# One block of an MLP product moved into the attention products, its second half packed in pairs, a fixed order, and two first loads on ScalarE's queue

## The chip, the cores and the metric

The kernel runs on one core of a Trainium2 chip. The metric is the device time in microseconds. The core's engines are TensorE (PE, matrix products; PEld is its weight load), VectorE (DVE), ScalarE (ACT), GpSimd (POOL) and SyncE (SP), which here issues the transfers (DMAs).

## The reference, cut to what matters

```python
def _A_ref(x, wqkv, wo):              # S=2048, D=512, H=32 heads of 16, W=8, dil=2
    qkv = (x @ wqkv) ...
    off = jnp.arange(W) * dil         # a token sees itself and 7 others, 2 apart
    logits = jnp.einsum("bhsd,bhswd->bhsw", q, kg) * scale
    ...
    o = jnp.einsum("bhsw,bhswd->bhsd", attn, vg)
    return o.transpose(...).reshape(B, S, D) @ wo
def _B_ref(x, w1, b1, w2, b2):        # F = 1376 = 10*128 + 96
    y = _layernorm(x, axis=-1)
    h = _gelu(jnp.einsum("bsd,df->bsf", y, w1) + b1)
    return jnp.einsum("bsf,fd->bsd", h, w2) + b2
x = A_x
xn = _layernorm(x, axis=-1)
s = _A_ref(xn, A_wqkv, A_wo)
g = _silu(_B_ref(xn, B_w1, B_b1, B_w2, B_b2))
return x + s * g
```

All inputs and outputs are float32.

## The kernel before, in words

Every operand of a product is split into two 16-bit parts, high and low, and a product is three matmuls: high by high, low by high, high by low. With the inner dimension of 512 in four parts of 128, a tile of an output takes 12 matmuls.

The 2048 tokens are taken as two parities c (a window with dilation 2 stays within one), each of 8 tiles of 128 tokens. First x is loaded, normalized, split and transposed to yT, some tiles by PE (line 683) and some by a transposing DMA (line 675). For two tiles ("FP", 6 and 7) a transposed copy of x is loaded too (line 1124, called t6 and t7), centred (a reduce on DVE at line 602, a small product at 608, a subtraction at 610), and multiplied by head block 0's weights in float32 directly (line 617), before anything is split.

The attention comes in 8 units: parity c by head block hb (8 heads, 384 columns of q, k and v). A unit's products (line 746) make 8 tiles of 12 matmuls into the product banks ps; ACT (line 763) or DVE (759) scales each out into U. DMAs copy halo rows of U (line 771), then DVE multiplies q by k (805), reduces (808), makes the softmax, multiplies by v (863, in the last unit 901), adds (858), and ACT and DVE split the result into high and low (846, 848); DMAs transpose it into oT (851). The output product with wo is line 929 for the first parity and line 961 for the last, whose results DVE scales and adds to x (993, 1000).

The MLP runs in 4 chunks (ch) of 512 tokens by NF = 11 blocks of F, the last of them 96 wide. The first product (mlp1, line 1016) makes a block transposed, features on partitions, in 12 matmuls of 512 columns; ACT does the gelu (1033) and the high part (1036), DVE the low part (1038). The second product (mlp2, line 1052) adds the block to four banks z, 3 matmuls each. The last block's h lies in a tile of its own, hlast, 97 rows: 96 features and a row that carries the bias b2. ACT's silu of z (1068, last chunk 1063) gives g, which goes through DRAM (gd) to the end.

The weights are brought to 16 bit at run time: loads (head blocks: load_q, line 505), sums of squares (514), a power of two as scale (qsc for head block 0), high parts (536) and low parts (543). At the start, small products of a constant tile (line 1169) keep PE busy.

A list scheduler in the class Plan sets the order on every engine: the code adds operations with an engine, an estimated duration, a priority and what they read and write, and the loop repeatedly places the one that the priorities and estimated times choose. Constants at the head of the file (priorities P..., engine choices such as HI_ENG, the order of the loads LOADS) feed it. Each engine then executes its list in that order.

Of the kernel before, what the change touches and what calls it, by code (L numbers as in the profile page):

```python
# [8 lines left out]
F32 = mybir.dt.float32  # L9
# [9 lines left out]
P = 128  # L19
# [14 lines left out]
LASTPOOL = (0, 2, 4)  # L34

# [3 lines left out]
LAG = 2  # L39

# [4 lines left out]
BYDMA = (4, 5, 6, 7)  # L45
TRZ = (3, 3, 0, 2, 0, 1, 1, 0)
PTR = (0.5487, 0.3388, 0.0342, 0.6565, 0.7826, 0.1978, 0.0549, 0.9)
GROUPS = ((0,), (1, 2), (3, 4, 5), (6, 7))
BATCHES = ((0, 1, 2, 3, 4, 5), (6, 7))
LOADS = (('t', 6), ('q', 0), ('q', 2), ('x', 2), ('x', 0), ('q', 4), ('t', 7), ('x', 5), ('x', 1), ('x', 3), ('x', 4), ('q', 6), ('w', 0), ('w', 2), ('x', 7), ('c', 2), ('s', 1), ('c', 0), ('w', 3), ('x', 6), ('w', 1), ('c', 1), ('b', 0), ('s', 0))  # L50
HI_ENG = ('act', 'act', 'act', 'dve', 'dve', 'dve', 'dve', 'act')
XT = (0, 4, 30, 34)
Y_ENG = ('pool', 'act', 'dve', 'dve', 'act', 'pool', 'dve', 'act')

W1ENG = ('act', 'dve', 'act', 'act', 'act', 'act', 'act')
# [3 lines left out]
W2LO = ('dve', 'dve', 'dve', 'dve', 'dve', 'pool', 'dve')  # L59
EV0 = ('act', 'dve', 'dve', 'act', 'act', 'act', 'dve', 'dve')  # L60
EV1 = ('dve', 'dve', 'act', 'act', 'act', 'act', 'dve', 'act')
QLO0 = ('pool', 'dve', 'dve', 'pool')
QLO1 = ('dve', 'dve')
W1LO = ('dve', 'dve', 'pool', 'dve', 'dve', 'dve', 'dve')
WOLAG = 2
MEANBY = ('dve', 'pe', 'pool', 'pool')
W2LATE = 6

BEFORE_W1 = (0, 1, 4, 5)

# [26 lines left out]
class Plan:  # L97
# [9 lines left out]
    def add(self, eng, dur, fn, reads=(), writes=(), prio=None, table=None, nbytes=0,  # L107
            after=None, holds=(), port=False, rate=350e3, issue=0.55, tail=1.4):
# [56 lines left out]
    def start(self):  # L165
        for o in self.ops:
            o.npred, o.ready, o.succs = len(o.preds), 0.0, []
        for o in self.ops:
            for p in o.preds:
                p.succs.append(o)  # L170
        self.free = {o.eng: 0.0 for o in self.ops}
        self.portfree, self.dma, self.landed, self.table = 0.0, 0.0, [], None

    def earliest(self, o):
        t = max(self.free[o.eng], o.ready)
        if o.port:
            t = max(t, self.portfree)
        if o.eng == "sp" and o.nbytes:
            left = FLIGHT
            for end, n in reversed(self.landed):  # L180
                left -= n
                if left < 0:
                    t = max(t, end)
                    break
        return t

    def place(self, o, t):

        if o.eng == "sp":
# [3 lines left out]
            self.dma = max(self.dma, t + o.issue + 0.3)  # L193
            self.dma += o.nbytes / (o.rate if self.dma > SLOW else 265e3)
            end = self.dma + o.tail
            self.landed.append((end, o.nbytes))
            return end
        end = t + o.dur
        if o.nbytes:
            self.free[o.eng] = end  # L200
            self.dma = max(self.dma, end + 0.3) + o.nbytes / o.rate
# [20 lines left out]
    def issue(self):  # L222
# [55 lines left out]
SLOW = 5.5  # L278

FLIGHT = 0.9e6  # L280

PW2 = 1.1284
PS2 = 0.4252
PWQ1 = 0.9
PW1 = 0.423
PB1 = 0.75
PCS = 0.6
PQ0 = 0.2677
PSQ0 = 0.1788
PMEAN = 0.04  # L290
PDIR = (0.192, 0.1517, 0.1187, 0.1556)
PG = (0.5671, 0.5205, 0.3952, 0.4033)
PY = (0.8339, 0.1477, 0.3649, 0.4824, 0.05, 0.5767, 0.05, 0.8333)
PU0 = 0.8687
PU1 = 0.969
PWARM = 0.9
PEV = 0.2698

PTOT = 0.5899

WAKE = 24
PS1 = 1.1561
# [3 lines left out]
PQLO = 0.5225  # L306

PFPLN = 0.35
PSEC = (0.6153, 0.7518, 0.1)

U1MH = 4
# [5 lines left out]
IORD0 = (6, 7, 0, 4, 1, 3, 2, 5)  # L317
IORD1 = (7, 0, 6, 3, 2, 4, 5, 1)
MLPN = (7, 7, 6, 4, 7, 7, 2, 0)
# [7 lines left out]
def tile_mixer(ctx, tc, a_x, a_xt, a_wqkv, a_wo, b_w1, b_b1, b_w2, out):  # L327
# [34 lines left out]
    ident = sb.tile([P, P], F32, name="ident")  # L362
    make_identity(nc, ident)
    fours = sb.tile([P, 2 * P], BF16, name="fours")
    nc.vector.memset(fours, 4.0)
    mean1 = sb.tile([P, P], F32, name="mean1")
    nc.vector.memset(mean1, 1.0 / D)
    halves = sb.tile([P, 16], F32, name="halves")
# [3 lines left out]
    misc = sb.tile([P, 512], F32, name="misc")  # L372
    v0 = misc[64:65]


    wq = sb.tile([P, NHB, 2, KT, 384], F16, name="wq")
    w1 = sb.tile([P, 2, KT * F], F16, name="w1")
# [6 lines left out]
    b1T = sb.tile([P, NF], F32, name="b1T")  # L384
    hlast = sb.tile([P, 2, 512], F16, name="hlast")
# [7 lines left out]
    R_mx = Ring(sb, [P, 64], F32, 4, "mx")  # L393
    R_cs = Ring(sb, [P, NI], F32, 8, "cs")
# [72 lines left out]
    def low_pool(n, lo, get, s, hi, **k):  # L467
# [4 lines left out]
        pool(0.45 + n * 3.9e-3, fn, **k)  # L472
# [25 lines left out]
    def k0(hb):  # L498
        return dict(rate=400e3, tail=0.6, issue=0.45) if hb == 0 else dict(tail=3.5) if hb > 1 else {}


    def load_q(hb, kk=range(0, KT, 2)):
        pre = pl.users([x for x in stkey[hb] if x is not xq0])
        for k in kk:
            dma(P * 3072, lambda k=k: nc.sync.dma_start(stq[hb]()[:, k * 384:(k + 2) * 384],
                                                        a_wqkv[hb, :, k * 384:(k + 2) * 384]),
                [], [("stq", hb, k), ("stq", hb, k + 1)] + stkey[hb], after=pre, **k0(hb))

    def scale_q(hb):
        col = R_s.new()  # L510
        for k in range(0, KT, 2):
            def go(k=k):
                src = stq[hb]()[:, k * 384:(k + 2) * 384]
                nc.scalar.activation(wq[:, hb, 0, k:k + 2].bitcast(BF16),
# [11 lines left out]
    def prep_q(hb):  # L526
# [3 lines left out]
        for k in range(0, KT, st):  # L530
            n = st * 384
            dst = [wq[:, hb, t, k:k + st].rearrange("p k e -> p (k e)") for t in range(2)]
            src = lambda k=k, n=n: stq[hb]()[:, k * 384:k * 384 + n]
# [17 lines left out]
    def factors(n, V, vs, mk, cdst, ckeys):  # L551
# [12 lines left out]
            rb.t[:, 0:n], p0b.t[:, 0:n], halves[:, 0:n], op=ALU.pow), [p0b], [(rb, 0)], port=False)  # L564
        with pl.fuse():
# [5 lines left out]
            cdst, a1(), halves[:, 8:8 + n], op=ALU.pow), [(A, 1)], ckeys, port=False)  # L571
# [53 lines left out]
    def ln0(g):  # L625
        q, n = cpos[g[0]], len(g)
        for i in g:
# [8 lines left out]
            rb0[:, q:q + n], pb0[:, q:q + n], halves[:, 0:n], op=ALU.pow), [("pb", g)], [("rb", g)], port=False)  # L636

    def second(g):
# [4 lines left out]
        with pl.fuse():  # L643
# [5 lines left out]
            cT[:, 0, q:q + n], x1, halves[:, 8:8 + n], op=ALU.pow), [("ab", g)], [("c", 0, i) for i in g], port=False)  # L649

    def y0(i):
# [12 lines left out]
        elif Y_ENG[i] == "pool":  # L664
            pool(1.25, lambda: nc.gpsimd.tensor_scalar(x(), x(), mv0[:, q, 0:1], rb0[:, q:q + 1], op0=ALU.subtract,
# [4 lines left out]
        if i in BYDMA:  # L670
# [6 lines left out]
                [y16, (y16, 0)] + [k for n in range(4) for k in s1k[n]], [("yh", 0, i), ("y", 0, i)], rate=140e3, issue=1.6, tail=1.2)  # L677
# [14 lines left out]
    def ln1():  # L692
# [13 lines left out]
        for i in range(NI):  # L706
# [10 lines left out]
                [y16, (y16, 0)], [("y", 1, i), ("yT", 2 + i // 4)], rate=1e6, issue=1.3)  # L717

    def qkv(c, hb, u):
# [13 lines left out]
        raw = pl.users([("xc", j) for j in FP]) if u == 1 else set()  # L735
        csk = {i: (cs, g) for g in parts for i in g} if u == 0 else {i: cs for i in range(NI)}
        for n, i in enumerate((IORD0, IORD1)[u] if u < 2 else IORD):
# [5 lines left out]
            def mm(n0=0, n1=12, y=y, o=o, b=b):  # L743
                for n in range(n0, n1):
                    (s, t), k = ((0, 0), (1, 0), (0, 1))[n // KT], n % KT
                    nc.tensor.matmul(b.t[:, 0:384], y[:, s, k, o:o + P], wq[:, hb, t, k],  # L746
# [5 lines left out]
            for n0, n1 in zip([0] + ends, ends):  # L752
                pe(n1 - n0, 384, lambda mm=mm, n0=n0, n1=n1: mm(n0, n1), [("yh" if n1 <= 4 else "y", c, i)] +
# [8 lines left out]
            else:  # L762
                act(384, lambda i=i, b=b: nc.scalar.activation(  # L763
                    U3[:, i:i + 31:15, :], b.t[:, 0:384].rearrange("p (t e) -> p t e", t=3),
                    AF.Identity, scale=cs.t[:, cp(i):cp(i) + 1]), **ev)

        ks = [("k", ub, i) for i in range(1, 8)]
        vs = [("v", ub, i) for i in range(1, 8)]
        for x, h, o, src in (("k", KH, KO, ks), ("v", VH, VO, vs)):
            for n, (a, b) in enumerate(HALO):  # L770
                dma((b - a) * 3584, lambda a=a, b=b, h=h, o=o: nc.sync.dma_start(
                    U3[a:b, h:h + 7, :], U3[a - 1:b - 1, o + 1:o + 8, :]), src,
                    [(x + "h", ub, n)], rate=300e3, issue=0.6)
        vrow = v0[0:1, hb * P:(hb + 1) * P]
        if c == 0:
            dma(512, lambda: nc.sync.dma_start(vrow, U3[0:1, VO, :]), vs + [("v", ub, 0)], [("v0", hb)])
# [3 lines left out]
            [("v0", hb), ("kz", ub)], [("vh0", ub)])  # L780
# [9 lines left out]
    def attention(c, hb, u):  # L790
# [51 lines left out]
        def emit_o(o, okeys, h0, h1):  # L842
# [12 lines left out]
                ([("s1a", n, 0) for n in range(2)] if u == 0 else []), rate=600e3, issue=1.6)  # L855
# [62 lines left out]
    def finish(c, i, t, tkey, x, eng="dve"):  # L918
# [4 lines left out]
        dma(P * 2048, lambda: nc.sync.dma_start(ov[c, i], t()), tkey[:1], [("out", c, i)], tail=0.7)  # L923
# [443 lines left out]
```

## Time and profile before

| what | value |
|---|---|
| time, median of 3 runs (lowest, highest) | 415.14 us (414.89, 415.17) |
| time of the profiled execution | 415.18 us |
| its span in the profile | 413.4 us |
| busy, share of the span: PE, DVE, ACT, POOL | 98%, 92%, 54%, 29% |
| granted PE clock | full in all 40 slices |
| bytes moved by DMA | 46.4 MB, 112 GB/s on average |

The span runs from the first to the last instruction; 1.78 us of the profiled time lie outside it. Busy time of PE is counted from the modelled ends of pipelined matmuls, so what a matmul costs is read from unbroken stretches. In the rows below, a group has its busy time and the mean of one in ns, then the idle time in front of it with what ended it.

### The profile page before, as it was taken

To read this page: it belongs to the slowest core of one execution; us is meant where nothing else is said; L and a number is where in the kernel's file an instruction comes from. 1 tells how busy PE (TensorE), PEld (TensorE's weight loads), DVE (VectorE), ACT (ScalarE), POOL (GpSimd) and SP (SyncE) were. 2 spreads that over 40 slices of the span, in tenths; PEclk is the share of its full clock that TensorE was granted. 3 is DMA by queue.
4 is the path that set the end of the run, shared out by engine and by line. 5 is a ranking of instruction groups with operands and counts; after the bars stand their busy time and mean duration, and the time that the engine had idled before them with its cause. 6 is when DMAs were issued, how large, how long until landed. Compare 5 with 4: busy or idle time off the path is not lost.

```text
span 413.4 us, 5554 instructions
## 1 busy us (share of the span) xinstructions
PE 405.9 (98%) x2083; PEld 206.6 (50%) x2083; DVE 379.5 (92%) x379; ACT 222.1 (54%) x353; POOL 120.3 (29%) x131
## 2 busy tenths in 40 slices
PE   8799999999999999999999999999999999999996
PEld 5555544445654455445544554455455544444443
DVE  4996989998999999989998999999999998999954
ACT  4699899994549655843384252225212393263500
POOL 3834002004380425042504330434033404520021
PEclk9999999999999999999999999999999999999999
DMA  8958717030045137720172034223604244007133
GB/s 281 397 112 258 235 61 230 0 128 1 1 142 152 28 93 183 149 46 2 48 221 75 0 102 116 68 86 88 205 7 122 88 111 145 0 18 238 23 102 131
DMA packets 47211, 46.41 MB, mean 112 GB/s; under 512 B 31785, under 2 KB 32225, under 8 KB 46673
## 3 DMA queue, kind: packets, MB, share of 16 engines
q1 hardware_dynamic: 47184, 46.06, 37.6%
q8 instruction: 16, 0.26, 0.3%
q14 instruction: 11, 0.08, 0.1%
HBM read 24.06 MB, written 7.34 MB: 76 GB/s over the span
## 4 chain that ended last, share of the span: by engine, by line
PE 92%; ACT 3%; issue 1%; DVE 1%; POOL 1%; ACTq 0%
PE z L1052 28%; PE ps L1016 28%; PE ps L746 25%; PE ps L929 5%; PE ps L961 2%; PE z L961 2%; PE pl L746 1%; ACT w L421 1%; PE pl L961 1%; ACT f L673 1%; ACT yT L687 0%; ACT wq L536 0%; POOL wq L471 0%; POOL rb L635 0%; ACT prod L661 0%
## 5 line engine op out<-in xcount | busy, mean ns | idle before, releaser
L1016 PE MATMUL ps<-yT,w 128*128 128x512 f16 (+1 forms) x528 | 120.4, 379 | 0.0
L746 PE MATMUL ps<-wq,yT 128*128 128x384 f16 x708 | 117.0, 326 | 0.2 <-DVE U L759 0.2
L1052 PE MATMUL z<-w,h 128*128 128x512 f16 x480 | 110.4, 379 | 0.0
L746 PEld LDWEIGHTS <-yT 128*128 128x128 f16 x744 | 72.5, 98 | 49.2 <-issue 1.0
L1016 PEld LDWEIGHTS <-w 128*128 128x128 f16 (+1 forms) x528 | 52.8, 100 | 61.0
L805 DVE TENSOR_TENSOR prod<-U 128x2048 f32<-128x2048 f32 x32 | 73.2, 2286 | 2.2 <-POOL prod L883 0.7
L1052 PEld LDWEIGHTS <-h 128*128 128x128 f16 x480 | 46.6, 98 | 55.5 <-issue 0.3
L808 DVE TENSOR_REDUCE L<-prod 128x128 f32<-128x2048 f32 x32 | 73.0, 2281 | 0.4
L1033 ACT ACTIVATE ps<-ps,b1T,hsc 128x512 f32<-128x512 f32 (+1 forms) x44 | 32.9, 748 | 73.4 <-PE ps L1016 72.2
L863 DVE TENSOR_TENSOR prod<-pl,U 128x2048 f32<-128x2048 f32 x28 | 63.2, 2283 | 4.2 <-POOL prod L873 4.1
L763 ACT ACTIVATE U<-ps,cs 128x384 f32<-128x384 f32 x54 | 31.2, 580 | 65.2 <-PE ps L746 65.2
L873 POOL TENSOR_TENSOR prod<-prod,prod 128x2048 f32<-128x2048 f32 x7 | 31.7, 4531 | 113.8 <-DVE prod L863 99.6
L883 POOL TENSOR_TENSOR prod<-prod 128x1024 f32<-128x1024 f32 x14 | 32.9, 2349 | 0.0
L882 POOL COPY gate<-prod 1x1 f32<-1x1 f32 x21 | 5.5, 264 | 91.0 <-DVE prod L805 82.2
L1038 DVE SCALAR_TENSOR_TENSOR h<-ps,hsc,h 128x512 f16<-128x512 f32 x40 | 29.6, 741 | 1.7 <-ACT h L1036 1.4
L1036 ACT ACTIVATE h<-ps,hsc 128x512 f16<-128x512 f32 x40 | 27.3, 684 | 1.3 <-PE z L1052 0.4
L929 PE MATMUL ps<-wo,oT 128*128 128x512 f16 x96 | 21.7, 379 | 0.0
L858 DVE TENSOR_TENSOR prod<-prod,prod 128x2048 f32<-128x2048 f32 x9 | 20.5, 2282 | 0.0
L1033 ACT ACT_TABLE_LOAD x10 | 12.8, 1283 | 8.6 <-PE ps L1016 8.5
L883 POOL TENSOR_TENSOR prod<-prod,prod 128x1024 f32<-128x1024 f32 x7 | 16.4, 2347 | 0.0
L961 PEld LDWEIGHTS <-oT 128*128 128x128 f16 x108 | 10.6, 98 | 10.4
L929 PEld LDWEIGHTS <-oT 128*128 128x128 f16 x96 | 9.4, 98 | 11.2
(179 smaller groups left out, 377.8 us busy)
## 6 DMA issues: line engine op xcount, KB each, us to landing
f<-in_A_x_dram SPq DMA_DIRECT2D x31, 256.0 KB, 3.5
U<-U SPq DMA_DIRECT2D x16, 392.0 KB, 4.0
gd<-f SPq DMA_DIRECT2D x12, 256.0 KB, 3.4
prod<-in_A_x_dram SPq DMA_DIRECT2D x8, 256.0 KB, 6.9
oT<-in_B_w_dram SPq DMA_DIRECT2D x2, 1024.0 KB
yT<-in_B_w_dram SPq DMA_DIRECT2D x2, 1024.0 KB, 7.9
f<-gd SPq DMA_DIRECT2D x8, 256.0 KB, 2.7
out_dram<-f SPq DMA_DIRECT2D x8, 256.0 KB, 2.8
```

What stands on the lines that cost most here:

```text
L746: nc.tensor.matmul(b.t[:, 0:384], y[:, s, k, o:o + P], wq[:, hb, t, k], start=(n == 0), stop=(n == 11))
L763: act(384, lambda i=i, b=b: nc.scalar.activation(U3[:, i:i + 31:15, :], b.t[:, 0:384].rearrange("p (t e) -> p t e", t=3), AF.Identity, sca ...
L805: dve(2048, lambda p2=p2, g=g: nc.vector.tensor_tensor(p2(), q, slots(Ut, KH, 2 * g), op=ALU.mult), qk + [("kh", ub, 0), ("kh", ub, 1), (" ...
L808: dve(2048, lambda pr=pr, g=g: nc.vector.tensor_reduce(L3()[:, 2 * g:2 * g + 2], pr.t.rearrange("p (r f d) -> p r f d", r=2, d=DH), AX.X, ...
L863: dve(2048, lambda: nc.vector.tensor_tensor(pr.t.rearrange("p (r f d) -> p r f d", r=2, d=DH), A3()[:, 2 * g:2 * g + 2].rearrange("p r (f ...
L873: pool(4.75, lambda: nc.gpsimd.tensor_tensor(acc.t, acc.t, p1.t, op=ALU.add), [acc, p1], [acc])
L883: nc.gpsimd.tensor_tensor(x.t[:, 0:1024], x.t[:, 0:1024], y(), op=ALU.add)
L929: nc.tensor.matmul(b.t, oT[:, hb, i // 4, s, i % 4], wo[:, t, hb], start=(hb == 0 and n == 0), stop=(hb == last and n == 2))
L961: nc.tensor.matmul(b.t[:, cols], oT[:, hb, i // 4, s, i % 4], wo[:, t, hb, cols], start=(start and hb == 0 and n == 0), stop=(stop and hb ...
L1016: nc.tensor.matmul(b.t[0:M], w1[:, s, f * 512 + k * M:f * 512 + (k + 1) * M], yT[ch][:, t, k], start=(n == 0), stop=(n == 11))
L1033: act(512, lambda: nc.scalar.activation(b.t[0:M], b.t[0:M], AF.Gelu_apprx_tanh, bias=b1T[0:M, f:f + 1], scale=hsc[0:M, 1:2]), [b, ("b1T",) ...
L1052: nc.tensor.matmul(z.t, hl[s][0:K, t * P:(t + 1) * P], w2[0:K, w, f], start=(f == 0 and n == 0), stop=(f == NF - 1 and n == 2))
```

## The change

**The last block of the MLP.** mlp1 no longer makes the 96-wide block. The last 96 columns of w1 (wl) are stored beside head block HLAST = 2's weights, whose products thus become 480 columns wide in both parities (line 864 after the change). ACT scales the 96 extra columns of each tile out into a tile hpt, hl0 for even chunks and first for odd (16 evictions, line 886). For each chunk, last_block then adds the bias on POOL, and does the gelu (line 818) and the high part (820) on ACT, the low parts on DVE in two pieces (827), and two transposing DMAs (833, 835). In mlp2 the last block's three matmuls per bank become, for each pair of banks, four of 128 rows (line 1172) and two of 34 rows (line 1175), one at partitions 0 to 33 and the other at 64 to 97. 128 rows hold the high part and a third of the low part, 34 rows the rest and the bias b2. The rows of w2 are laid out accordingly (w2t, lomask, hrem).

**The order.** A table ORDER with the numbers of all 1264 operations replaces the scheduler's choice, and most constants are new. Among them: the centring for the FP tiles goes by small products and no longer by the reduce on DVE; other x tiles are transposed by DMA (2, 5, 6, 7 where it was 4, 5, 6, 7); most high parts of w1 go to DVE.

**The first loads.** The two loads of head block 0's weights are issued by ScalarE's queue; SP starts with x tiles and t6.

```diff
     def load_q(hb, kk=range(0, KT, 2)):
         for k in kk:
-            dma(P * 3072, lambda k=k: nc.sync.dma_start(stq[hb]()[:, k * 384:(k + 2) * 384],
-                                                        a_wqkv[hb, :, k * 384:(k + 2) * 384]),
+            q = nc.scalar if hb == 0 else nc.sync
+            pl.add("act" if hb == 0 else "sp", 0.42 if hb == 0 else 0.0,
+                   lambda k=k, q=q: q.dma_start(stq[hb]()[:, k * 384:(k + 2) * 384],
+                                                a_wqkv[hb, :, k * 384:(k + 2) * 384]),
...
-        order = []
+        order, fixed = [], [self.ops[n] for n in reversed(ORDER)]
         while len(order) < len(self.ops):
             best = None
-            for e, cand in engs.items():
+            if fixed:
+                o = fixed.pop()
+                t = max([self.earliest(o)] + [min(b.ring.free) for b in o.bufs if b.slot is None])
+                best = (t, o)
+            for e, cand in engs.items() if best is None else ():
...
-BYDMA = (4, 5, 6, 7)
+BYDMA = (2, 5, 6, 7)
-W1ENG = ('act', 'dve', 'act', 'act', 'act', 'act', 'act')
+W1ENG = ('dve', 'dve', 'act', 'dve', 'dve', 'act', 'dve')
-MEANBY = ('dve', 'pe', 'pool', 'pool')
+MEANBY = ('pe', 'pe', 'pe', 'dve')
+ORDER = (
+    8, 0, 121, 128, 118, 124, 132, 131, 113, 112, 125, 134, 129, 114, 127, 122, 19, 116, 117, 52, 53, 55, 56,
...
     def qkv(c, hb, u):
+        wide = 384 + FL * (hb == HLAST)
...
-                    nc.tensor.matmul(b.t[:, 0:384], y[:, s, k, o:o + P], wq[:, hb, t, k],
+                    nc.tensor.matmul(b.t[:, 0:wide], y[:, s, k, o:o + P], wq[hb][:, t, k],
...
+            if hb == HLAST:
+                act(FL, lambda i=i, b=b: nc.scalar.activation(
+                    hpt[i // 4][:, (i % 4) * FL:(i % 4 + 1) * FL], b.t[:, 384:384 + FL], AF.Identity, scale=hsc[:, 1:2]),
...
+        for j in range(2 if hb == HLAST else 0):
+            last_block(2 * c + j)
...
+    def last_block(ch):
+            pool(1.0, lambda: nc.gpsimd.tensor_tensor(x3(), x3(), row, op=ALU.add), xk + [("b1T",)], xk)
+            act(n, lambda: nc.scalar.activation(x, x, AF.Gelu_apprx_tanh), xk, xk,
...
+            low(lambda: v()[:, :, :, FL:P], 0, 2 * FR, (h16, 1))
+            low(lambda: hrem.rearrange("p a b (o f) -> p (a b) o f", o=2)[:, :, 0:1, 0:FR], 2 * FR, FL, ("hreml",))
...
     def mlp2(ch, f):
+            def pair(a=a, z=list(zt)):
+                ha = hlt[ch % 2].rearrange("p a (t x) -> p (a t) x", t=4)
+                for t in range(a, a + 2):
+                    for w in range(2):
+                        nc.tensor.matmul(z[t].t, ha[:, 2 * t + w], w2[:, w, f], start=False, stop=False)
+                for t in range(a, a + 2):
+                    r = slice(64 * (t - a), 64 * (t - a) + FR + 2)
+                    nc.tensor.matmul(z[t].t, hlc[ch % 2][r, a // 2], w2t[r], start=False, stop=True)
...
-            if p < len(steps):
+            if p < len(steps) and steps[p][1] < NF - 1:
                 with prio(PR_M + p * 10):
                     mlp1(*steps[p])
```

Three places in the order. The first is SP's list at the very start; t6 is the first load from in_A_xt, in_A_wqkv is head block 0's weights (in prod) and then others (in U), in_A_x are the x tiles. Before:

```order
L1124 DMA U_87<-in_A_xt_dram 128x512
L505 DMA prod_93<-in_A_wqkv_dram 128x768 x2
L1099 DMA prod_94<-in_A_x_dram 128x512 x2
L505 DMA U_87<-in_A_wqkv_dram 128x768
L1124 DMA U_87<-in_A_xt_dram 128x512
```

After:

```order
L1231 DMA prod_100<-in_A_x_dram 128x512
L1256 DMA U_94<-in_A_xt_dram 128x512
L1231 DMA prod_102<-in_A_x_dram 128x512
L1231 DMA prod_100<-in_A_x_dram 128x512
L1256 DMA U_94<-in_A_xt_dram 128x512
```

Head block 0's two loads are gone from SP's list, and an x tile now stands ahead of t6. The two loads stand at the head of ACT's list, ahead of its table load and the sums of squares that read them:

```order
L588 DMA prod_101<-in_A_wqkv_dram 128x768 x2
L597 ACT_TABLE_LOAD
L597 ACTIVATE wq_82,s_125<-prod_101 128x768 x2
L770 CAST yT_89<-z_149 128x4x128
L742 ACTIVATE rb_155<-pb_154,rb_155 128x1
L744 ACTIVATE prod_100<-prod_100,rb_155 128x512
L619 ACTIVATE wq_82<-prod_101,qsc 128x384 x3
```

The second place is PE's list at the last block of the first chunk's second product; z00, z10, z20 and z30 are the banks, hlast, hl0 and tail hold the block's rows. Before, three matmuls follow one another for each bank:

```order
L1052 LDWEIGHTS hlast_91
L1052 MATMUL z00_143<-w2_80,hlast_91 128x512
L1052 LDWEIGHTS hlast_91
L1052 MATMUL z00_143<-w2_80,hlast_91 128x512
L1052 LDWEIGHTS hlast_91
L1052 MATMUL z00_143<-w2_80,hlast_91 128x512
```

After, two full matmuls for each bank of a pair, then the packed two:

```order
L1172 MATMUL z20_149<-w2_87,hl0_98 128x512
L1172 LDWEIGHTS hl0_98
L1172 MATMUL z30_150<-w2_87,hl0_98 128x512
L1172 LDWEIGHTS hl0_98
L1172 MATMUL z30_150<-w2_87,hl0_98 128x512
L1175 LDWEIGHTS tail_78
L1175 MATMUL z20_149<-tail_78 128x512
L1175 LDWEIGHTS tail_78
L1175 MATMUL z30_150<-tail_78 128x512
```

The packed pair goes to two banks, from two row ranges of the same tile.

The third place is ACT's list around the last head block's evictions (U_87 before, U_94 after; ps are the product banks), which stand in the order of PE's products. Before:

```order
L763 ACTIVATE U_87<-ps_140,cs_120 128x3x128
L763 ACTIVATE U_87<-ps_141,cs_120 128x3x128
L763 ACTIVATE U_87<-ps_139,cs_120 128x3x128
L763 ACTIVATE U_87<-ps_140,cs_120 128x3x128
L763 ACTIVATE U_87<-ps_141,cs_120 128x3x128
L763 ACTIVATE U_87<-ps_139,cs_120 128x3x128
L846 ACTIVATE o_105<-prod_94,osc 128x2x512
L1033 ACTIVATE ps_140<-ps_140,b1T,hsc 128x512
```

After:

```order
L882 ACTIVATE U_94<-ps_143,cs_123 128x3x128
L1154 ACTIVATE ps_143<-ps_143,b1T,hsc 128x512
L882 ACTIVATE U_94<-ps_145,cs_123 128x3x128
L882 ACTIVATE U_94<-ps_144,cs_123 128x3x128
L1157 ACTIVATE h_115<-ps_143,hsc 128x512
L971 ACTIVATE o_112<-prod_100,osc 128x2x512
L956 ACT_TABLE_LOAD
L956 ACTIVATE L_110<-L_110 128x512
L1200 ACT_TABLE_LOAD
L1200 ACTIVATE f_109<-z_147,zsc 128x512
L1200 ACTIVATE f_107<-z_149,zsc 128x512
L882 ACTIVATE U_94<-ps_144,cs_123 128x3x128
```

The eighth tile's eviction has moved behind a gelu, a softmax step and two silus; the matmuls of other work stand between the seventh and the eighth tile on PE in the same way.

More of the change, by code (lines that the diff above doesn't have):

```diff
@@ L107, in add @@
     def add(self, eng, dur, fn, reads=(), writes=(), prio=None, table=None, nbytes=0,
-            after=None, holds=(), port=False, rate=350e3, issue=0.55, tail=1.4):
+            after=None, holds=(), port=False, rate=390e3, issue=0.45, tail=0.8):
         if self.fused is not None and eng == self.fused["eng"]:
@@ L178, in earliest @@
         if o.eng == "sp" and o.nbytes:
[L179 to L184, printed above, removed]
+            if len(self.landed) >= FLIGHT:
+                t = max(t, self.landed[-FLIGHT])
         return t
@@ L383, in tile_mixer @@
     cT = sb.tile([P, DIL, NI], F32, name="cT")
-    b1T = sb.tile([P, NF], F32, name="b1T")
-    hlast = sb.tile([P, 2, 512], F16, name="hlast")
+    b1T = sb.tile([P, NF + FL], F32, name="b1T")
+    hl0 = sb.tile([P, 512], F32, name="hl0")
+    hpt = [hl0[:, 0:512], first[:, 0:512]]
+    hlt = [h.bitcast(F16).rearrange("p (a t) -> p a t", a=2) for h in hpt]
     gd = dr.tile([DIL, NI, P, D], F32, name="gd")
@@ L1161, in tile_mixer @@
             y0(i)
-    for kind, i in LOADS:
+    for kind, i in list(LOADS) + [("c", 3), ("c", 4)]:
         if kind in "sc":
```

287 lines of the change are left out of this document (176 added, 111 removed), and 61 rows, old and new, of the table ORDER.

## The prediction

> **What bounds the kernel now.** I read the head of the page first, then the windows, TensorE's waits, the groups by form, the chain, and last the timeline at both ends.
>
> ```profile
> span 413.4 us, 5554 instructions
> ...
> PE 405.9 (98%) x2083; PEld 206.6 (50%) x2083; DVE 379.5 (92%) x379; ACT 222.1 (54%) x353; POOL 120.3 (29%) x131
> ...
> PEclk9999999999999999999999999999999999999999
> ...
> PE 92%; ACT 3%; issue 1%; DVE 1%; POOL 1%; ACTq 0%
> ```
>
> TensorE is busy for 98% of the span and is 92% of the chain that ended last, at full clock throughout. DVE is second at 92%. The profiled execution took 415.18 us, 1.78 more than its span, and the median of three runs is 415.14, so a change of the span can be set against either. 0.2%, which is about what a measurement of this kernel can tell from no change, is 0.83 us.
>
> ```profile
> core 0: us, PE busy (x) PEld busy (x) DVE busy (x) ACT busy (x) POOL busy (x), PEclk, DMA share, GB/s
> ...
> 5.00:10.00 5.00, 4.88 (x20) 2.76 (x20) 2.97 (x11) 2.44 (x7) 0.00 (x0) 1.00 0.99 358
> 10.00:15.00 5.00, 3.35 (x20) 2.40 (x21) 4.78 (x11) 3.30 (x8) 3.25 (x4) 1.00 1.04 413
> 15.00:20.00 5.00, 4.52 (x29) 2.79 (x28) 4.79 (x19) 3.12 (x6) 4.92 (x6) 1.00 1.04 410
> ...
> 46.40:100.00 53.60, 53.60 (x256) 24.66 (x255) 50.22 (x56) 46.69 (x92) 6.92 (x9) 1.00 0.32 102
> ...
> 300.00:395.00 95.00, 95.00 (x466) 46.00 (x464) 90.12 (x67) 40.38 (x53) 24.50 (x26) 1.00 0.29 82
> ```
>
> From 46.4 us on TensorE has no idle time until the end. Its slack lies at the start: between 5 and 20 us it is busy for 4.88 + 3.35 + 4.52 = 12.75 of 15 us, while the DMA engines are full. So a matmul taken out of the middle is worth its whole time, provided that DVE's 50.22 of 53.6 and 90.12 of 95 us keep up.
>
> **The change, part by part.** First the paces. The mean of a matmul in the groups is its latency, so pace is taken from unbroken stretches of the chain.
>
> ```profile
> 101.60 15.60 PE ps L746 x96
> ...
> 119.14 2.59 PE ps L1016 x12
> ```
>
> A 384-column matmul costs 15.60/96 = 162.5 ns, a 512-column one 2.59/12 = 216 ns.
>
> ```profile
> L1052 PE MATMUL z<-w,h 128*128 128x512 f16 x480 | 110.4, 379 | 0.0
> ...
> L1052 PE MATMUL z<-w,hlast 97*128 97x512 f16 x48 | 11.0, 379 | 0.0
> L1016 PE MATMUL ps<-yT,w 128*96 128x512 f16 x48 | 11.0, 379 | 0.0
> ```
>
> *(a) The 96-column block of the first MLP product goes:* 48 matmuls x 216 ns = -10.4 us.
>
> *(b) One head block becomes 480 columns wide:* 2 units x 8 tiles x 12 = 192 matmuls get 96 columns more. By the two paces a column costs (216 - 162.5)/128 = 0.42 ns, so 96 cost 40 ns: 192 x 40 = +7.7 us. No 480-column matmul is in the trace; between the two measured widths I see nothing that would make it dearer. These products now also wait for the cast of w1's last columns (priced in e), which is issued some ten rows into ACT's list, long before this head block.
>
> *(c) The second product's last block:* before 48 matmuls of 97 rows, after 32 of 128 rows and 16 of 34 rows, which come in 8 pairs on two different row groups. If a pair runs at once, 8 x 216 ns = 1.73 us go. If the rows of a pair cannot overlap and each passage into and out of the packed form lets the pipeline run empty, 16 passages cost at most the latency less the pace, 379 - 216 = 163 ns, or 2.6 us: a balance of +2.6 with no overlap, +0.9 with it. The nearest row is the 97-row group: 11.0/48 = 229 ns, beside 110.4/480 = 230 ns for full rows, so fewer rows by themselves cost nothing. I take -1.2 and keep -1.7 to +2.6. A rule speaks against it: the Trainium skill, "TensorEngine Tiling (Array Packing)", section "Key Properties", says that changing the tiling mode drains TensorE. By that rule this term would be +0.9 and not -1.2; no row of before has two row groups, so nothing here shows which.
>
> *(d) The start.*
>
> ```profile
> 0.73 0.39 SPq L1124 DMA_DIRECT2D U<-in_A_xt_dram  x1
> 1.18 0.89 SPq L505 DMA_DIRECT2D prod<-in_A_wqkv_dram  x2
> ...
> 3.57 1.02 DVE L602 TENSOR_REDUCE f<-U 128x128 f32<-128x512 f32 x1 [2.29 <-DMA U<-in_A_xt_dram]
> ...
> 4.49 0.84 ACT L514 ACTIVATE wq<-prod 128x768 bf16<-128x768 f32 x1 [2.48 <-DMA prod<-in_A_wqkv_dram]
> ...
> 6.22 1.62 PE L617 MATMUL pl<-prod,U 128*128 128x384 f32 x4
> 6.84 0.84 ACT L514 ACTIVATE wq<-prod 128x768 bf16<-128x768 f32 x1 [1.41 <-DMA prod<-in_A_wqkv_dram]
> 7.49 0.70 DVE L576 BATCH_NORM_STATS2 bn<-prod 128x6 f32<-128x512 f32 x1 [1.32 <-DMA prod<-in_A_x_dram]
> ...
> 19.54 4.71 PE L746 MATMUL ps<-wq,yT 128*128 128x384 f16 x28
> ```
>
> SP issues the transposed tile t6 first, then the two halves of head block 0, then the x tiles, about 0.45 us each; what waits for them starts at 3.57, 4.49, 6.84 and 7.49. After the change ScalarE issues the two halves at the same time as SP issues x1 and then t6. The bytes are the same: one t, two q and one x tile land by 7.49 in either case. But they no longer land one behind the other. If the four share the engines, each lands near the end of the lot, t6 at about 6.8 and not 3.57. Before, 2.65 us lie between t6 and the first direct product (6.22 - 3.57), of which a reduce on DVE (1.02) now gives way to small products on PE; so the first direct product comes at about 8.4, some 2.2 us later. That meets the 15 - 12.75 = 2.25 us of slack between 5 and 20, so most is absorbed: as the direct products and the scaling of q0 are also in the way of ACT's later work, I take +0.7. Its bounds: -1, if t6 is hardly late and x1, now landing first, lets tile 1 be transposed earlier; +4, if the delays of t6 and of the scale add up with none of the slack left. ACT's queue is not hurt by the issues themselves: two cost 0.89 us on SP and ACT's first work waits 2.48 us for their data.
>
> *(e) Side work.*
>
> ```profile
> L763 ACT ACTIVATE U<-ps,cs 128x384 f32<-128x384 f32 x54 | 31.2, 580 | 65.2 <-PE ps L746 65.2
> ...
> L1038 DVE SCALAR_TENSOR_TENSOR hlast<-ps,hsc,hlast 96x512 f16<-96x512 f32 x4 | 3.0, 744 | 1.9 <-ACT hlast L1036 1.9
> L1033 ACT ACTIVATE ps<-ps,b1T,hsc 96x512 f32<-96x512 f32 x4 | 3.0, 743 | 17.2 <-PE ps L1016 17.2
> ...
> L1036 ACT ACTIVATE hlast<-ps,hsc 96x512 f16<-96x512 f32 x4 | 2.7, 680 | 0.1
> ...
> L726 ACT ACTIVATE cs<-cT,qsc 128x8 f32<-128x8 f32 x7 | 1.7, 290 | 2.9 <-POOL cT L570 2.5 <-DVE qsc L459 0.4
> ```
>
> ACT loses 4 gelus and 4 casts (3.0 + 2.7 us) and gains 16 evictions of 96 columns, each between the 290 ns of the 8-column row and the 580 of the 384-column one (4.6 to 9.3 us), 4 gelus of 384 columns (2.3 at 580) and 4 casts of 768 (3.4 at the 0.84 us of ACT's 768-column rows above): +4.6 to +9.3 us, against 53.6 - 46.69 = 6.9 us free in the densest stretch of 53.6 us and 54.6 free between 300 and 395. DVE loses 3.0 us and gains 8 lows, 4 of them small and none above 744 ns. Four bias additions go to POOL, which is busy for 6.92 of 53.6 us. The two transposes per chunk go by SP, and their reader, the second product's last block, stands last in its chunk. What TensorE can feel is the product bank: each 96-column eviction holds one up to 0.58 us longer, 16 x 0.58 = 9.3 us if all were waited for, but a tile's 12 matmuls take 2.4 us and its two evictions at most 1.16. TensorE's longest wait for a bank before is this:
>
> ```profile
> PE ps L746 <- DVE U L759: 0.2, 1, 0.2
> ```
>
> The new order cuts the work into smaller pieces on all engines, so I put new waits at +0.8 us, four such waits, bounds 0 and 3 (five of the 0.58).
>
> **Sum.** -10.4 + 7.7 - 1.2 + 0.7 + 0.8 = -2.4: span 411.0, time 412.8 us. The forecast's own range is 411.8 to 414.2.
>
> **The rivals.** *(1) DVE becomes the bound at the end.*
>
> ```profile
> 308.49 15.76 PE L746 MATMUL ps<-wq,yT 128*128 128x384 f16 x96
> ...
> 327.67 2.28 DVE L805 TENSOR_TENSOR prod<-U 128x2048 f32<-128x2048 f32 x1
> ...
> 392.97 0.75 DVE L848 SCALAR_TENSOR_TENSOR o<-prod,osc,o 128x512 f16<-128x512 f32 x1 [0.79 <-ACT o L846]
> ...
> 398.56 0.81 PE L961 MATMUL pl<-wo,oT 128*128 128x512 f16 x3
> ...
> 408.29 1.47 PE L961 MATMUL ps<-wo,oT 128*128 128x256 f16 x12
> ```
>
> The last head block's 96 matmuls stand in one piece before and end at 324.3, 85.5 us ahead of TensorE's end (409.8). In the new table 60 other matmuls stand between its seventh and eighth tiles, 60 x 216 ns = 13 us, and the matmuls left behind the eighth come to 69.7 us by the two paces. On DVE the attention of that head block takes from 327.67 to 393.72, 66.05 us, from its first product to its last split. The new order takes some 9 us of work on earlier units out of that stretch, which leaves 57. With TensorE's end at 407.2 the eighth tile is done at 337.5 and evicted at 338.1, and DVE at 395.3. How long the last output then takes to be transposed lies between the landing of a plain load of 256 KB and the 4.84 us that passed before from the last split to its first reader, which did not wait:
>
> ```profile
> f<-gd SPq DMA_DIRECT2D x8, 256.0 KB, 2.7
> ```
>
> So it is there between 398.0 and 400.1; its first reader stands 6.5 us ahead of the end, at 400.7. The slack is 0.6 to 2.7 us, say 1.6. For this rival: DVE has little idle time to catch up in, the table moves casts of w1 from ACT to DVE, and the fetch of halo rows behind the eviction (DMA) is not in these numbers. Against it: the products of the other head blocks stand ahead of that first product and can cover the fetch. It decides from 4 us of lateness, where the time passes 415.14; 6 us give 412.8 + (6 - 1.6) = 417.2. *(2) The start eats the gain:* the four loads land as late as above and ACT, which casts, normalizes and scales one behind another in 16 to 28 us, passes it on; (d) is +3 and not +0.7, giving 415.1. The Trainium skill, "DMA: Bandwidth & Descriptors", section "Issuing engines are not separate DMA queues", says that loads issued by several engines interleave on the same 16 engines and that only issue time is saved; the DMA share of 0.99 in 5 to 10 us agrees that there is no bandwidth left to win. *(3) The packed pairs stall:* each passage lets the pipeline run empty, (c) is +0.9 with overlap, giving 414.9; this is the outcome of the rule on tiling modes above. *(4) More gain:* t6 hardly late and no new waits: (d) -0.3 and (e) 0 give -10.4 + 7.7 - 1.2 - 0.3 = -4.2, 411.0.
>
> **How the numbers follow.** Forecast 0.41, more gain 0.17, start 0.11, packed stall 0.08, DVE 0.23. The start and stall cases lie mostly within 0.2% (0.16) and for the rest above (0.03). So faster 0.58, same 0.16, slower 0.26. The range leaves out the half of the DVE case that runs on past 417, and the edge of the case of more gain: 410.4 to 417.0. The likeliest time is 412.8.
>
> **What would show it.** Right: no group of 96-column first products, the widened group at about 0.2 us a matmul in unbroken stretches, TensorE's idle time after 46 us below 2 us, direct products from about 8.4. (c) is read from how long two packed matmuls take beside full ones. The DVE rival shows as a wait of the last output products for the transposed outputs, the start rival as TensorE reaching its unbroken stretch 3 us later. I am wrong if the packed pairs stall or if waits spread through the middle.

## The result and the profile after

| | before | after |
|---|---|---|
| time, median (lowest, highest) | 415.01 us (414.81, 415.17) | 418.99 us (418.57, 419.20) |
| ratio to before, 95% interval | | 1.0095 (1.0077 to 1.0112) |
| span of the profiled execution | 413.4 us | 416.8 us |

The change makes the kernel 4 us slower, where a gain, to 412.8 us, was forecast. In the medians below, two of the six runs of the version under "All three" (420.8 and 420.9 us) and one of the six with more dummy products (424.4 us) were in a slower state of the chip and are left out. The head of the page of the changed kernel:

```profile
span 416.8 us, 5512 instructions
...
PE 403.9 (97%) x2041; PEld 200.3 (48%) x2041; DVE 383.5 (92%) x388; ACT 224.4 (54%) x373; POOL 134.8 (32%) x139
```

TensorE's list is shorter, as meant, but the span is 3.4 us longer. Its waits in the changed kernel, then in the kernel before (line waited for, us in total, times, longest):

```profile
PE z L1172 <- DMA hl<-f: 2.7, 1, 2.7
PE ps L682 <- DMA U<-in_A_xt_dram: 2.3, 1, 2.3
...
PE ps L864 <- DVE h L1159: 0.4, 1, 0.4
```

```profile
PE z L683 <- POOL prod L665: 1.6, 1, 1.6
...
PE z L683 <- DVE prod L668: 0.4, 1, 0.4
```

The second product's last block waits 2.7 us for its transposed rows (hl), and the first small products wait 2.3 us for t6. Neither wait was there before; two waits at the start, of 1.6 and 0.4 us, are gone. The rows of the end, from the timelines of the changed kernel and of the kernel before:

```profile
404.85 8.98 SPq L1127 DMA_DIRECT2D out_dram<-U  x9
...
409.11 1.47 PE L1086 MATMUL ps<-wo,oT 128*128 128x256 f16 x12
...
411.04 0.75 DVE L1125 TENSOR_TENSOR U<-U 128x256 f32<-128x256 f32 x2
```

```profile
399.60 11.50 SPq L1002 DMA_DIRECT2D out_dram<-U  x9
...
410.32 0.42 DVE L1000 TENSOR_TENSOR U<-U 128x256 f32<-128x256 f32 x1
```

TensorE ends at 410.58 (409.76 before), and 6.22 us follow until the span ends (3.64 before). SP's last store is issued by 413.83, 2.0 us after the last add; before by 411.10, 0.4 us after it. So the account of the span is: TensorE's end +0.8, what follows it +2.6, together +3.4.

TensorE's own +0.8 comes of these rows. The pace of the widened products and the packed block, in the chain and in the timeline of the changed kernel:

```profile
110.87 7.30 PE ps L864 x36
```

```profile
207.60 1.03 PE L1172 MATMUL z<-w,first 128*128 128x512 f16 x4
208.56 0.39 PE L1175 MATMUL z<-tail 34*128 34x512 f16 x2
208.88 1.04 PE L1172 MATMUL z<-w,first 128*128 128x512 f16 x4
...
210.18 1.15 PE L864 MATMUL ps<-wq,yT 128*128 128x384 f16 x6
```

A 480-column matmul takes 7.30/36 = 202.8 ns, 40.3 more than one of 384: (a) and (b) hold, -10.4 + 7.7 = -2.7. Four full matmuls start at 207.60 and the pair at 208.56, 0.96 later: 4 x 0.216 and 0.10 more. The pair is over in 0.32: one matmul's 0.216 and again 0.10. By these times alone two matmuls one behind the other, without any such price, would fit as well (0.42 against 2 x 0.216); but both together last 0.39, and a single one lasts 0.386, so the second starts with the first. The two do run at once, and each passage (from full to packed matmuls or back) costs 0.10 us. The twelve take 2.58 us, and unpacked they would take 12 x 0.216 = 2.59. (c) is -0.1: 16 x 0.10 less 1.73. With the waits of 2.7 and 0.4 in the middle, the start is left with 0.8 + 2.7 + 0.1 - 3.1 = +0.5; this term is what remains, and not measured by itself.

### The profile page after: what moved, and what is told of

Same layout as the page of the kernel before. It is cut to its first block, busy times and chain, and to the rows that moved or that the text cites. A ratio compares the mean times of both kernels' runs of the same rounds, so it can differ in the third digit from the quotient of the medians.

```text
span 416.8 us, 5512 instructions
## 1 busy us (share of the span) xinstructions
PE 403.9 (97%) x2041; PEld 200.3 (48%) x2041; DVE 383.5 (92%) x388; ACT 224.4 (54%) x373; POOL 134.8 (32%) x139
## 4 chain that ended last, share of the span: by engine, by line
PE 87%; DVE 5%; ACT 4%; DMA 1%; issue 1%; SPq 0%; DVEq 0%
PE ps L864 29%; PE z L1184 22%; PE ps L1141 22%; PE ps L1054 5%; PE z L1086 2%; PE ps L1086 2%; DMA U<-in_A_xt_dram 1%; PE z L1172 1%; DVE prod L988 1%; PE pl L864 1%; DVE h L1159 1%; PE pl L1086 1%; ACT wq L619 1%; DVE L L933 1%; DVE prod L930 1%
## 5 line engine op out<-in xcount | busy, mean ns | idle before, releaser
L864 PE MATMUL ps<-wq,yT 128*128 128x384 f16 (+1 forms) x720 | 129.7, 337 | 0.4 <-DVE h L1159 0.4
L1184 PE MATMUL z<-w,h 128*128 128x512 f16 x480 | 111.8, 379 | 0.0
L1141 PE MATMUL ps<-yT,w 128*128 128x512 f16 x480 | 108.8, 379 | 0.0
L1141 PEld LDWEIGHTS <-w 128*128 128x128 f16 x480 | 46.7, 98 | 55.4 <-issue 0.5
L998 POOL TENSOR_TENSOR prod<-prod,prod 128x2048 f32<-128x2048 f32 x7 | 39.5, 5640 | 59.1 <-DVE prod L988 59.1
L1154 ACT ACTIVATE ps<-ps,b1T,hsc 128x512 f32<-128x512 f32 x40 | 29.5, 745 | 34.6 <-PE ps L1141 34.5
L971 ACT ACTIVATE o<-prod,osc 128x1024 f16<-128x1024 f32 (+1 forms) x9 | 9.5, 1051 | 12.5 <-DVE prod L983 7.0
L1122 POOL TENSOR_TENSOR U<-U,f 128x512 f32<-128x512 f32 x3 | 4.1, 1394 | 35.0 <-DVE U L1118 32.3
```

The source lines that it names most:

```text
L864: nc.tensor.matmul(b.t[:, 0:wide], y[:, s, k, o:o + P], wq[hb][:, t, k], start=(n == 0), stop=(n == 11))
L998: pool(4.75, lambda: nc.gpsimd.tensor_tensor(acc.t, acc.t, p1.t, op=ALU.add), [acc, p1], [acc])
L1141: nc.tensor.matmul(b.t[0:M], w1[:, s, f * 512 + k * M:f * 512 + (k + 1) * M], yT[ch][:, t, k], start=(n == 0), stop=(n == 11))
L1154: act(512, lambda: nc.scalar.activation(b.t[0:M], b.t[0:M], AF.Gelu_apprx_tanh, bias=b1T[0:M, f:f + 1], scale=hsc[0:M, 1:2]), [b, ("b1T",) ...
L1184: nc.tensor.matmul(z.t, hl[s][:, t * P:(t + 1) * P], w2[:, w, f], start=(f == 0 and n == 0), stop=False)
```

## The experiments

All are compared with the kernel before on the same chip, whose median was 414.8 to 415.0. What an edit is worth is its median's distance from 418.99, the changed kernel's; the interval of a ratio reaches, in most, some 0.6 us to either side.

**The order of the stores.** In the table, the last nine stores were put in the order in which their data are ready:

```diff
-    ..., 1262, 1239, 1234, 1244, 1254, 1259, 1229, 1263, 1249, 1224,
+    ..., 1262, 1224, 1239, 1229, 1254, 1234, 1244, 1249, 1259, 1263,
```

> Only the order of the last nine output stores on SP's list is changed: they go out in the order in which their data were ready in the trace, so that no ready store stands behind a later one. Theory (the end was lengthened by the order of the stores): after the changed kernel's last VectorE add at 411.8 us of the span, the span ended 5.0 us later, before it was 2.7 us; with the stores in order the end should come 2.7 us after the last add again: -2.3 us, to about 416.7. Rival (the end is late because TensorE and VectorE end late, the stores follow): at most 0.5 us gain.

Measured: 416.77 us, ratio 1.0045 (1.0030 to 1.0059); the span is 414.9. In its timeline TensorE and DVE end as before the edit, and SP ends 1.3 us earlier:

```profile
404.42 8.06 SPq L1127 DMA_DIRECT2D out_dram<-U  x9
...
409.23 1.47 PE L1086 MATMUL ps<-wo,oT 128*128 128x256 f16 x12
...
411.16 0.75 DVE L1125 TENSOR_TENSOR U<-U 128x256 f32<-128x256 f32 x2
```

Worth 2.2 us with nothing else changed: the theory held. In the table of the change the store of the first tile, whose add was done at 404.3 on POOL, was the very last on SP's list; of two other full tiles that were ready, one stood between the two half tiles that end last and one behind both. SP's list is executed in order, so three full tiles went out behind the first of these half tiles.

**The late remainder.** What makes the transposes late is seen in the timeline of the changed kernel:

```profile
122.42 4.62 POOL L998 TENSOR_TENSOR prod<-prod,prod 128x2048 f32<-128x2048 f32 x1 [0.59 <-DVE prod L988]
122.59 4.61 DVE L827 SCALAR_TENSOR_TENSOR hrem<-hl,hsc,f 128x128 f16<-128x128 f32 x1
...
127.78 1.28 SPq L833 DMA_TRANSPOSE hl<-f  x1
...
131.22 1.02 PE L1172 MATMUL z<-w,hl 128*128 128x512 f16 x4 [2.69 <-DMA hl<-f]
...
132.67 0.34 DVE L827 SCALAR_TENSOR_TENSOR hrem<-first,hsc,f 128x128 f16<-128x128 f32 x1
```

The same instruction takes 0.34 us for the next chunk. In chunk 0 it stood beside POOL's 2048-wide add and ended 0.16 us after it, and the code lets both transposes wait for it. The first experiment moved only this instruction away, to POOL ahead of that add:

```diff
-            low(lambda: hrem..., 2 * FR, FL, ("hreml",))
+            if ch == 0:
+                def low_pool():
+                    xr = x3()[:, :, 2 * FR:FL]
+                    nc.gpsimd.tensor_scalar(xr, xr, hsc[:, 2:3], 1.0, op0=ALU.mult, op1=ALU.mult)
+                    nc.gpsimd.tensor_tensor(rest(), xr, v()[:, :, 0, 2 * FR:FL], op=ALU.subtract)
...
```

> In chunk 0 alone, the low part of the last 32 of the 96 columns is made on GpSimd (a scaling in place and a subtraction) and not on VectorE, where it took 4.61 us beside GpSimd's add of 4.62 us (0.34 us in the next chunk). Theory (that collision delayed the two transposes, and TensorE waited 2.7 us for them): the transposes are issued some 4 us earlier, the wait of the second product's last block disappears: -2.5 to -2.9 us, to about 416.2. Rival (the transposes are late for another reason, SP's queue or their own 3.4 us to land): wait and time stay within 0.5 us.

Measured: 418.77 us, ratio 1.0091 (1.0077 to 1.0105). The wait for hl is gone, the time is not. Timeline, then TensorE's waits:

```profile
122.75 4.83 DVE L1412 TENSOR_SCALAR f<-f,zsc 98x512 f32<-98x512 f32 x1
122.77 4.52 POOL L1006 TENSOR_TENSOR prod<-prod,prod 128x2048 f32<-128x2048 f32 x1
123.01 1.30 SPq L841 DMA_TRANSPOSE hl<-f  x1
```

```profile
PE ps L872 <- DVE h L1167: 2.1, 2, 1.4
...
PE z L1180 <- DVE w L1406: 0.7, 1, 0.7
```

The next VectorE instruction in the row stood beside the add instead (0.47 us in the changed kernel, 4.83 here). DVE lost the same 4.3 us, and TensorE waited for DVE at two other lines. Here the expectation was wrong in taking the transposes for the loss: they were only the first to need DVE's time.

**Holding the add.** The second experiment left VectorE's work alone and held POOL's add of this head block (the second, u = 1) back, by a one-element copy that reads VectorE's first product of the third:

```diff
+            def first_add():
+                if u == 1:
+                    nc.gpsimd.tensor_copy(gate, held[0].t[0:1, 0:1])
+                nc.gpsimd.tensor_tensor(acc.t, acc.t, p1.t, op=ALU.add)
...
```

> GpSimd's 2048-wide add of the second head block (4.6 us) is held by a small copy that reads VectorE's first product of the third head block, so it starts some 10 us later, behind the VectorE work that it stood beside (4.61 us for a 128x128 remainder; when that was moved away, 4.83 us for a 98x512 scaling right behind it). Theory (GpSimd's add and a VectorE instruction on two SBUF operands exclude each other, VectorE lost 4.3 us there and both waits of TensorE, 2.9 us for the transposes and 0.5 us for a product bank, come from that): no such VectorE instruction is long any more and TensorE's idle time between 120 and 150 us falls from 3.4 us to under 1: -2.5 to -3.4 us, about 416. Rival (VectorE has too much work there in any case, or GpSimd's late add makes a new wait): the same idle time at another place, as when the remainder alone was moved; within 0.7 us.

Measured: 415.49 us, ratio 1.0017 (1.0004 to 1.0030). In the timeline the remainder takes 0.34 us, the add starts at 134.1 us, and TensorE has no wait left after the start:

```profile
122.51 0.34 DVE L827 SCALAR_TENSOR_TENSOR hrem<-hl,hsc,f 128x128 f16<-128x128 f32 x1
...
123.45 1.29 SPq L833 DMA_TRANSPOSE hl<-f  x1
...
134.13 4.53 POOL L1003 TENSOR_TENSOR prod<-prod,prod 128x2048 f32<-128x2048 f32 x1
```

```profile
PE ps L682 <- DMA U<-in_A_xt_dram: 2.4, 1, 2.4
PE z L1309 <- DVE first L438: 1.2, 1, 1.2
```

Worth 3.5 us: one collision of 4.3 us on DVE made both waits. The planner counts such instructions of DVE and POOL as exclusive (portfree in the class Plan): in its times one begins where the other ends. But nothing in the program holds the engines to that. POOL's list is run in order as the data come, and the add's data, VectorE's two products right ahead of these instructions, came first. The Trainium skill, "SBUF — State Buffer", section "Who interferes with whom", calls the ports that DVE and GpSimd share an exclusive lock for a whole instruction, won by whichever issues first. The rows agree: POOL began at 122.42, DVE's instruction at 122.59, and it ended at 127.20, 0.16 us after POOL's.

**The packed pairs.** First they were taken apart, each packed matmul behind its own two full ones:

```diff
                 for t in range(a, a + 2):
                     for w in range(2):
                         nc.tensor.matmul(z[t].t, ha[:, 2 * t + w], ...)
-                for t in range(a, a + 2):
                     r = slice(64 * (t - a), 64 * (t - a) + FR + 2)
                     nc.tensor.matmul(z[t].t, hlc[ch % 2][r, a // 2], w2t[r], ...)
```

> The same matmuls, but each packed matmul stands behind its own two full ones, so that no two packed ones stand side by side: 32 passages into and out of the packed form and not 16, and no overlap. Theory of the trace (a passage costs 0.1 us, a pair side by side runs at once): 8 x (0.216 + 0.2) = +3.3 us. The prediction's term (passages cost nothing, a pair overlaps): +1.7 us less what was not overlapped, +1.2. If passages cost 163 ns each: 8 x (0.216 + 0.33) = +4.3 us.

Measured: 425.43 us, ratio 1.0228 (1.0191 to 1.0264), 6.4 us above the changed kernel: more than any of the three forecasts. Chunk 1 in the timeline, then the first matmuls of chunk 0's block and the window around them:

```profile
212.64 0.59 PE L1172 MATMUL z<-w,first 128*128 128x512 f16 x2
213.17 0.39 PE L1174 MATMUL z<-tail 34*128 34x512 f16 x1
213.49 0.60 PE L1172 MATMUL z<-w,first 128*128 128x512 f16 x2
...
216.06 0.99 PE L864 MATMUL ps<-wq,yT 128*128 128x384 f16 x5
```

```profile
131.44 1.01 PE L1172 MATMUL z<-w,hl 128*128 128x512 f16 x2 [2.67 <-DMA hl<-f]
```

```profile
130.00:140.00 10.00, 8.56 (x19) 1.86 (x20) 9.97 (x11) 3.88 (x6) 0.00 (x0) 0.56 0.52 99
```

In chunk 1 the block takes 216.06 - 212.64 = 3.42 us, 0.84 more than packed side by side; four chunks make +3.4, as 0.10 a passage says. The rest comes from chunk 0, where the granted clock is 0.56 from 130 to 140 us. The order of the matmuls did not bring it down: the first two full ones behind the wait, ahead of any packed one, already take 1.01 us (0.59 in chunk 1). In the changed kernel the same wait is followed by four in 1.02. From 131.44 us on, the block and the 24 matmuls behind it lose some 4.5 us to the clock in the profiled execution, which took 426.13 us: 3.4 + 4.5, less a wait of 0.4 that is gone, make 7.5, and it lies 7.6 above the changed kernel's 418.57. Why the same wait lowers the clock in one kernel and not in the other stays open. So the run shows the price of a passage in its rows, and not by its time alone.

Then, on top of the mends below, the four packed products of chunks 0 to 2 were put together behind the eight full ones (10 passages, not 16):

> The same three mends, and in chunks 0 to 2 the four packed products of the last block stand together behind the eight full ones, so that there are 10 passages into and out of the packed form and not 16. Theory (0.1 us each): 0.6 us below the kernel with the three mends alone, 411.4 to 412.2. Rival (what a passage costs is hidden, or the later end of two banks makes a wait): no difference, or up to 0.4 us more.

Measured: 410.50 us against 411.94 without it, ratio to before 0.9897 (0.9882 to 0.9912). Chunk 0 in its timeline:

```profile
126.31 1.89 PE L1181 MATMUL z<-w,hl 128*128 128x512 f16 x8
128.13 0.61 PE L1184 MATMUL z<-tail 34*128 34x512 f16 x4
128.67 1.68 PE L1148 MATMUL ps<-yT,w 128*128 128x512 f16 x7
```

The four packed ones are over in 0.54 us, two pairs of 0.216 and a passage; without overlap they would take 0.86. The twelve take 2.36 us and not 2.58, that is 0.2 a chunk or 0.6 in all, as expected. The median fell by 1.4; the other 0.8 us are in the start. At the first 24 unbroken matmuls of the second product the profiled execution stands at 57.67 us, and without the edit at 58.41, though the lists up to there are the same. With the edit ACT reads head block 0's first half at 5.50 us, without it at 7.08. Why it landed sooner isn't known.

**The first loads.** Head block 0's loads were given back to SP, behind x1 and t6:

```diff
-            q = nc.scalar if hb == 0 else nc.sync
-            pl.add("act" if hb == 0 else "sp", 0.42 if hb == 0 else 0.0,
+            q = nc.sync
+            pl.add("sp", 0.0,
```

> Head block 0's two loads are issued by SP again, behind x1 and t6, all else and the table as they are. Theory (the start is nearly neutral: at 20 us TensorE had 386.3 us of matmuls left, 0.5 more than before less what the change took out): within 0.7 us of the changed kernel, t6 lands earlier (4 to 5 us and not 6.6) and TensorE's clock stays up in 5 to 15 us, but the loads of head block 0 land later by about as much. Rival (the late t6 and the lowered clock cost the start 2 to 3 us): -2 to -3 us, to about 416.5.

Measured: 417.57 us, ratio 1.0058 (1.0043 to 1.0072): 1.4 us, between the two. First products and head block 0's loads in the timeline of the changed kernel, and of this one; then the windows of 5 to 10 us, in the same order:

```profile
5.28 0.84 ACT L597 ACTIVATE wq<-prod 128x768 bf16<-128x768 f32 x1 [2.33 <-DMA prod<-in_A_wqkv_dram]
...
6.65 1.27 PE L682 MATMUL ps<-U,first 128*128 128x128 f32 x8 [2.34 <-DMA U<-in_A_xt_dram]
6.91 0.84 ACT L597 ACTIVATE wq<-prod 128x768 bf16<-128x768 f32 x1 [0.69 <-DMA prod<-in_A_wqkv_dram]
```

```profile
4.13 2.06 PE L682 MATMUL ps<-U,first 128*128 128x128 f32 x8
6.84 0.84 ACT L597 ACTIVATE wq<-prod 128x768 bf16<-128x768 f32 x1 [4.83 <-DMA prod<-in_A_wqkv_dram]
...
7.91 0.84 ACT L597 ACTIVATE wq<-prod 128x768 bf16<-128x768 f32 x1
```

```profile
5.00:10.00 5.00, 3.35 (x17) 2.85 (x18) 4.06 (x8) 2.43 (x5) 1.34 (x2) 0.76 1.06 385
```

```profile
5.00:10.00 5.00, 3.73 (x20) 2.50 (x19) 3.05 (x5) 2.34 (x5) 0.99 (x2) 1.00 0.97 334
```

On SP, t6 is there 2.5 us earlier, and head block 0's halves are read 1.6 and 1.0 us later. TensorE waited for t6, so the sharing lost. How much is seen at the first 24 unbroken matmuls of the second product, in the chains of the changed kernel and of this one:

```profile
59.72 5.18 PE z L1184 x24
```

```profile
58.25 5.18 PE z L1184 x24
```

They start 1.5 us earlier. Whether the change lost by t6 or by the clock that fell in the idle time was tried with ten more dummy products ahead of the wait:

```diff
-        pl.add("pe", 0.2, lambda b=b: nc.tensor.matmul(...), ...)
+        pl.add("pe", 0.2, lambda b=b, n=n: [nc.tensor.matmul(...) for _ in range(11 if n == 122 - 112 else 1)], ...)
```

> Ten more of the small dummy products stand on TensorE ahead of its first wait for t6, about 2.1 us of them, so that it does not sit idle there; the loads stay on ScalarE's queue. Theory (what the start loses is the granted clock, 0.76 and 0.90 in 5 to 15 us after 2.3 us of idle time, and not the late t6 itself): the clock stays at 1.00 and the time falls by 1 us or more, as with the loads back on SP (-1.4). Rival (it loses by the late t6): the clock stays up and the time stays within 0.4 us.

Measured: 418.99 us, ratio 1.0101 (1.0078 to 1.0124). The clock stayed at 1.00 and the time did not move, so it is the late t6:

```profile
5.00:10.00 5.00, 4.52 (x26) 3.12 (x25) 3.90 (x8) 2.46 (x5) 1.34 (x2) 1.00 1.05 398
```

In the profiled execution the same 24 matmuls start at 59.16 us, 0.6 earlier, so the clock may have a small part. The run that held the add speaks against it: there the clock was 1.00 in 5 to 15 us, behind a wait of 2.4 us and without more dummies, and they start at 59.65.

**All three.** Stores in order, the add held, loads on SP:

> The three mends together: stores in order of readiness, GpSimd's add held, head block 0's loads on SP. Theory (three separate losses: 2.2, 3, 1.4 us): they add up to -6.2 to -7 us against the changed kernel, 412.0 to 412.8, that is 2.2 to 3 us faster than before. Rival (behind one loss stands the next, VectorE's work): -3.6 us, 415.4, no faster than before.

Measured: 411.94 us, ratio 0.9928 (0.9913 to 0.9944). That is 7.0 us below the changed kernel; singly they gave 2.2 + 3.5 + 1.4 = 7.1. With the packed products together this is the version at 410.50 that beats both kernels. Last, that version with ScalarE's queue again:

> The kernel with the three mends and the packed products together, but head block 0's loads on ScalarE's queue as in the change: the queue is the only difference from the run before it in this list. Theory (the loads on ScalarE's queue cost the start 1.4 us whatever stands behind): 411.9 us, still faster than before by some 3 us. Rival (the 1.4 us came from a VectorE collision or store order that shifted with the start): within 0.5 us of 410.5.

Measured: 413.21 us, ratio 0.9962 (0.9937 to 0.9986), 2.7 us above the version on SP. The queue's price is there too, and larger than expected. It is paid at the start: the 24 matmuls start at 60.28 us and not at 57.67. Of these 2.6 us, 0.7 are the better start that only the version on SP just before has and that isn't explained, and 0.5 are a wait for a product bank that it does not have:

```profile
PE ps L683 <- DMA U<-in_A_xt_dram: 2.3, 1, 2.3
...
PE ps L1148 <- ACT U L883: 0.5, 1, 0.5
```

## Why the prediction was wrong, by its own steps

- **(a) and (b)** held: 202.8 ns for the widened matmul, -2.7 us together.
- **(c)** was mis-sized: -1.2 taken, -0.1 measured. The 97-row group, which I took as the nearest row, has no packed pairs, and says nothing of passing between forms. A passage costs 0.10 us, under the 163 ns that I had as its bound. The rule that I set against it, the Trainium skill, "TensorEngine Tiling (Array Packing)", section "Key Properties", that changing the mode drains TensorE, agrees in that a passage has a price.
- **(d)** was forecast with +0.7, and +0.5 is left in the account; t6 came at 6.65 (I had 6.8), the first direct product at 9.2 (8.4). But the near hit is luck: the reason I gave for a small price, that slack takes it up, was at most half right, since the loads back on SP gain 1.4 us. The rest of the new order of the start is then some 0.9 us better than the old one, and the queue takes more than that away. The slack was misread too: the 12.75 us that I counted as busy hold some 1.9 us of the constant tile's products, which can give way.
- **(e)** is one of the two steps that failed. Its 0.8 us of new waits rested on free time of the engines and on the reader of the transposes standing last in its chunk. 3.1 us came, from one collision of DVE and POOL. I had summed DVE's work and POOL's work, each against its own free time, and not asked which of the new DVE instructions stands beside a POOL add.
- **The end** is the other. The sum ran to TensorE's end and took what follows as unchanged, without a term. It grew by 2.6 us, and 2.2 of them are the order of the stores on SP's list, which the prediction does not read.
- **Rival 1 (DVE at the end)** did not happen: TensorE has no wait behind 150 us, though the eighth tile came late as described. **The start rival** had its mechanism, at less than half its price (1.4 us for the queue, against 3). **The packed rival** had the right mechanism and a size of -0.1 and not +0.9.

With the measured terms the sum is -2.7 - 0.1 + 0.5 + 3.1 + 2.6 = +3.4, the span's growth; since the +0.5 is what remains, the sum closes by construction. The range ended at 417.0. New waits had a bound of 3 us in (e), but no chance of their own; the end was no case at all. Without its 2.6 us the time would have been 416.4, inside the range and still slower than before.

## What to carry to other kernels

When an order is fixed by a table, read each engine's list to its last row, that of the queue that stores the results too: a store that is ready but stands behind the last one lengthens the kernel, here by 2.2 us for three of 256 KB. An order holds within one engine only. Where a plan counts on two engines to take turns, look for what in the program makes them, and if there is nothing, a one-element copy that reads the other's result does. And when a wait is mended and the time does not move, look at what the engine behind it lost, not at the wait.

## What the runs showed of the hardware

- A DVE instruction of 0.34 us lasted 4.61 beside a POOL add of 4.62, and one of 0.47 lasted 4.83.
- Two matmuls of 34 rows on different row groups run at once (0.39 us for both, 0.386 for one), and each passage to or from that form costs 0.10 us (0.96 and 0.32 us between starts, 0.216 a matmul).
- A wait of the same length did not always lower the granted clock. Behind 2.7 us it was 1.00 in the changed kernel and 0.50 (131.4 to 138 us) with the packed products apart, from the first full matmul on. At the start, behind 2.3 to 2.4 us, it was 0.76 in 5 to 10 us in the changed kernel and 1.00 in the one that held the add. What decides isn't shown.
